# Holding the later loads back, and issuing weights earlier, in the start-up of a fused SSD and ReGLU kernel

## The chip, the cores and the metric

The kernel runs on one core of a Trainium2 chip. The metric is device time in microseconds, the median over several executions. A profiled execution gives the trace: which engine did what and when, how busy the 16 DMA engines of the core were, and which clock TensorE (the matmul engine) was granted. The other engines are VectorE (DVE in the profile), ScalarE (ACT), GpSimd (POOL) and SyncE (SP, which here only issues transfers).

## The reference, cut to what matters

Two stages follow each other. The first is a chunked state-space recurrence ("SSD") over 4 batches, 8 heads, 768 positions, head size 32 and state size 16; the second is a gated feed-forward layer on the result.

```python
# x: (4,8,768,32)  a: (4,8,768)  B, C: (4,8,768,16); chunk = 32
cum = cumsum(log a) within the chunk
L   = exp(cum_i - cum_j), lower triangle
y   = (C B^T * L) x  +  exp(cum_i) * C state
state = exp(sum log a) * state + sum_j exp(cum_end - cum_j) B_j x_j^T
# then, with x = y as (3072, 256), w_gate and w_val (256,1536), w_out (1536,256)
out = (maximum(x @ w_gate, 0) * (x @ w_val)) @ w_out
```

All inputs and the output are float32.

## The kernel before, in words

The kernel works on chunks of 128 positions, two at a time: a "pair" is 256 positions of one batch with all 8 heads, so there are 12 pairs and 3 per batch. The feed-forward layer works on blocks of 512 rows (two pairs) and 12 column blocks of 128 (`f` from 0 to 11). The decay is folded into B and C: both are multiplied by factors that come from running products of `a`, and what is left is a plain masked product.

For a pair p the steps are these. `load_bc` and `load_x` (or `load`) bring B, C and x into SBUF, all on SP's queue apart from some of the first ones, which ScalarE issues. `scale_wide` multiplies C (j = 1) or B (j = 0) by the factors, in two instructions each, on VectorE for pair 0 and on GpSimd for pairs 1 and 2. `cast_x` makes x bfloat16. `turn` transposes C and then B on TensorE, and `tevac` copies the result out of PSUM (tiles CT and BT). `G_wide` makes the products of C and B in four PSUM banks, `adds` the chunk's contribution to the state (it reads the cast x), `gmask` and `gcopy` mask and move the products, `carry` and `pass_on` hand the state on, `inter_wide` and `D_wide` make the output of the pair, and `yevac_wide` writes it transposed into yT.

`gvh(b, f, u)` is one column block of the first feed-forward product for half a row block (256 rows): two matmuls with the gate weights `wg`, two with the value weights `wv`, a ReLU on ScalarE and a product on VectorE. `gv` does the same for 512 rows. `fout` and `foevac` make the output. All of them share five PSUM banks.

The weights are read by GpSimd's queue, which also turns them into bfloat16: `weights(f0, f1)` issues one transfer for wg and one for wv, of 256 KB each for four column blocks; `weights_out` loads `w_out`.

The order of instructions on every engine is the order of the program: `in_order` adds a dependency from each instruction to the one before it on its engine. Each engine then runs its list strictly in turn, and an issue of a transfer is an instruction in the list of the engine that issues it. So the program text after line 623 is the schedule. `load_x(1, ...)` has one addition: it first sets one element of its tile by a `memset` on VectorE (line 94), and since the load overwrites that element, SP's issue waits for VectorE to get to this place in its list. All that follows on SP waits behind it.

The stretch at hand is the start-up: pair 0 goes through all its steps, pair 1 follows, and the first feed-forward blocks are put between them. In the program of before:

```python
    halves(0, 0, 0, 1)                       # column blocks 0, 1 of pair 0
    G_wide(1)
    adds(1)
    ...
    late = [gvh(0, 2, 0, True), gvh(0, 3, 0, True)]
    ...
    late += [gvh(0, 4, 0, True), gvh(0, 5, 0, True)]
    inter_wide(1)
    D_wide(1)
```

Of the kernel before, what the change touches and what calls it, by code (L numbers as in the profile page):

```python
# [29 lines left out]
def kernel(  # L30
# [13 lines left out]
    nc = tc.nc  # L44
# [34 lines left out]
    def load_bc(p, j, *qs):  # L79
        s = st.setdefault(p, {})  # L80
        if "bcr" not in s:
            s["bcr"] = raw.tile([128, NH, 2, 2, N], FP32, tag="bcr", name="bcr")
        n = NH // len(qs)
        for i, q in enumerate(qs):
            hs = slice(i * n, (i + 1) * n)
            q.dma_start(
                out=s["bcr"][:, hs, j].rearrange("p h r n -> p h (r n)"),
                in_=(B, C)[j][0, hs, p * 256:(p + 1) * 256, :].rearrange(
                    "h (p r) n -> p h (r n)", r=2))

    def load_x(p, *qs):
        xr = raw.tile([128, NH, 2, D], FP32, tag="xr", name="xr")
        if p == 1:
            nc.vector.memset(xr[0:1, 0, 0, 0:1], 0.0)
        n = NH // len(qs)
        for i, q in enumerate(qs):
            hs = slice(i * n, (i + 1) * n)
            q.dma_start(out=xr[:, hs].rearrange("p h r d -> p h (r d)"),
                        in_=x[0, hs, p * 256:(p + 1) * 256, :].rearrange(
                            "h (p r) d -> p h (r d)", r=2))  # L100
        st.setdefault(p, {})["xr"] = xr

    def load(p):
        q = nc.sync
        if p < NWIDE:
            load_bc(p, 1, q)
            load_bc(p, 0, q)
            load_x(p, q)
            return
        b, c0 = p // PPB, 2 * (p % PPB)  # L110
        xr = raw.tile([128, 2, NH, D], FP32, tag="xr", name="xr")
        bcr = raw.tile([128, 2, 2, NH, N], FP32, tag="bcr", name="bcr")
        for i in range(2):
            sl = slice((c0 + i) * 128, (c0 + i + 1) * 128)
            for src, j in ((B, 0), (C, 1)):
                q.dma_start(out=bcr[:, i, j], in_=src[b, :, sl, :].rearrange("h s n -> s h n"))
            q.dma_start(out=xr[:, i], in_=x[b, :, sl, :].rearrange("h s d -> s h d"))
        st[p] = {"xr": xr, "bcr": bcr}
# [69 lines left out]
    def weights(f0, f1):  # L188
        fs = slice(f0 * 128, f1 * 128)
        for w, src in ((wg, moe_w_gate), (wv, moe_w_val)):  # L190
            nc.gpsimd.dma_start(  # L191
                out=w[:, :, fs], in_=src[:, fs].rearrange("(k p) f -> p k f", k=2))
# [74 lines left out]
    def scale_wide(p, j, eng):  # L267
        s = st[p]
        if "bs" not in s:
            s["bs"] = bs = att.tile([128, 4, 128], BF16, tag="bs", name="bs")  # L270
            s["tin"] = [[bs[:, 2 * j + r] for r in range(2)] for j in range(2)]
        src = s["bcr"].rearrange("s (t q) j r n -> s j r t q n", t=2)[:, j]
        f = wfac[:, j, :, :, p]
        for t in range(2):
            eng.tensor_tensor(
                out=s["bs"][:, 2 * j:2 * j + 2].rearrange(
                    "s k (q t n) -> s k t q n", q=4, t=2)[:, :, t],
                in0=src[:, :, t],
                in1=f[:, :, 4 * t:4 * t + 4].to_broadcast([128, 2, 4, N]),
                op=ALU.mult)  # L280
# [16 lines left out]
    def cast_x(p, ceng):  # L297
        s = st[p]
        cast = ceng.copy if ceng is nc.scalar else ceng.tensor_copy
        xb = att.tile([128, 2 * NH * D], BF16, tag="xb", name="xb")  # L300
        if p < NWIDE:
            cast(xb, s["xr"].rearrange("s h r d -> s (h r d)"))
            s["xb"] = xb.rearrange("s (h r d) -> s h r d", h=NH, r=2)
        else:
            cast(xb, s["xr"].rearrange("s i h d -> s (i h d)"))
            s["x"] = [xb[:, i * NH * D:(i + 1) * NH * D] for i in range(2)]

    def transp(p, k, apart=False):

        s = st[p]  # L310
        if "tp" not in s:
            s["tp"] = {}
        if apart and k == 0:
            s["tp"][k] = bank("tpb", (128, 2, 128), BF16)
        elif not s["tp"]:
            tp = mm.tile([128, 2, 2, 128], BF16, tag="tp", name="tp")
            s["tp"] = {0: tp[:, 0], 1: tp[:, 1]}
        for i in range(2):
            nc.tensor.transpose(out=s["tp"][k][:, i], in_=s["tin"][k][i], identity=ident)  # L319
# [45 lines left out]
    def gmask(p, q, eng, psum=False):  # L365
        s = st[p]
        d = s["gw"][:, q]
        m = wmask.unsqueeze(2).to_broadcast([128, 2, 2, 128])
        eng.tensor_tensor(out=d, in0=s["gp"][q] if psum else d, in1=m, op=ALU.mult)

    def gcopy(p, q):
        s = st[p]
        nc.scalar.copy(out=s["gw"][:, q], in_=s["gp"][q])
# [259 lines left out]
    scale_wide(0, 1, V)  # L633
    nc.vector.reciprocal(wfac[:, 0, :, :, 0], wfac[:, 1, :, :, 0])
    scale_wide(0, 0, V)
    load_x(1, nc.sync)
    load(2)
    load(3)
    transp(0, 1, False)
    keep_warm(3)  # L640
    transp(0, 0, True)
    tevac(0, A_, V)
    nc.vector.reciprocal(wfac[:, 0, :, :, 1:3], wfac[:, 1, :, :, 1:3])
    scale_wide(1, 1, P_)
    scale_wide(1, 0, P_)
    weights(4, 8)
    cast_x(0, A_)
    keep_warm(4)
    G_wide(0)
# [1 line left out]
    keep_warm(19)  # L651
    gcopy(0, 0)
    gmask(0, 2, V, True)
    gcopy(0, 1)
    gmask(0, 3, V, True)
    gmask(0, 0, V)
# [192 lines left out]
```

## Time and profile before

| what | us |
|---|---|
| median of 7 runs (lowest to highest) | 131.19 (130.76 to 132.87) |
| the profiled execution's own time | 131.81 |
| its span | 130.1 |
| TensorE busy in the span | 122.3 |
| VectorE, ScalarE, GpSimd busy | 88.5, 81.9, 40.2 |
| mean granted TensorE clock | 0.987 of full speed |

Times in the trace count from the start of the span. In the timeline a row is start, duration, engine, line of the program, operation, output and inputs, and in brackets how long the engine sat idle before it and what ended that. A row can stand for several instructions (x2). "SPq" and "POOLq" are issues of transfers by SP and GpSimd; a transfer's landing is counted from its issue. The chain of waits goes back from the last instruction to what released it at each step. In the DMA view q0 is GpSimd's queue and q1 is SP's.

### The profile page before, as it was taken

The numbers are of one execution on the slowest core, as the hardware profiler recorded it, in microseconds if no ns is written. First come the engines' busy times: TensorE is split into PE (matmuls) and PEld (weight loads), VectorE is DVE, ScalarE is ACT, GpSimd is POOL, SyncE is SP. The second block draws the span as 40 slices with busy tenths as digits, with TensorE's granted clock in tenths as the row PEclk, the third lists the DMA queues.
The fourth block names the chain that finished last, engine by engine and source line by source line (L and its number), as shares of the span: only waits on it lengthen the run. The fifth ranks groups of instructions, "written<-read, shape, count | busy, mean of one in ns | idle before, by whom it ended". The sixth has DMA issues, their size and how long they took to land.

```text
span 130.1 us, 3446 instructions
## 1 busy us (share of the span) xinstructions
PE 122.3 (94%) x1294; PEld 85.0 (65%) x1294; DVE 88.5 (68%) x200; ACT 81.9 (63%) x186; POOL 40.2 (31%) x84
## 2 busy tenths in 40 slices
PE   6983999999999999999999999999999999999990
PEld 6751568667678567785558884477865577854770
DVE  4773675976399977468766778665799775687410
ACT  0554657863598874588744798844887845876310
POOL 6569941005375003390003670002930032000000
PEclk9999779999999999999999999999999999999999
DMA  4999999989797993269940186772200002200031
GB/s 71 200 178 195 208 196 205 108 96 128 81 168 136 117 104 51 85 121 122 103 63 27 53 156 73 96 88 83 86 0 0 0 5 81 81 0 5 0 109 53
DMA packets 72208, 12.14 MB, mean 93 GB/s; under 512 B 65936, under 2 KB 72192, under 8 KB 72192
## 3 DMA queue, kind: packets, MB, share of 16 engines
q1 hardware_dynamic: 66096, 8.91, 44.7%
q0 software_dynamic: 3184, 2.36, 12.2%
q10 hardware_dynamic: 2912, 0.66, 2.4%
q8 instruction: 10, 0.16, 0.5%
q14 instruction: 6, 0.05, 0.2%
HBM read 11.13 MB, written 3.15 MB: 110 GB/s over the span
## 4 chain that ended last, share of the span: by engine, by line
PE 86%; DMA 7%; DVE 2%; ACT 1%; POOL 1%; issue 0%; DVEq 0%; ACTq 0%
PE o L598 25%; PE gv L580 21%; PE gate L562 14%; PE val L565 14%; DMA wv<-in_moe_w_val_dram 6%; PE y L537 2%; PE g L463 2%; PE tp L319 2%; DMA a<-in_a_dram 2%; PE A_ps L500 1%; PE y L526 1%; POOL wg L191 1%; DVE h L586 1%; PE dec L246 1%; PE g L356 1%; ACT r L583 1%
## 5 line engine op out<-in xcount | busy, mean ns | idle before, releaser
L598 PE MATMUL o<-wo,h 128*128 128x256 bf16 x288 | 34.7, 273 | 0.0
L569 DVE TENSOR_TENSOR h<-r,val 128x512 bf16<-128x512 bf16 x42 | 28.3, 684 | 7.4 <-ACT r L568 6.4
L586 DVE TENSOR_TENSOR h<-r,gv 128x256 bf16<-128x256 bf16 x60 | 23.8, 420 | 10.0 <-ACT r L583 9.6
L598 PEld LDWEIGHTS <-h 128*128 128x128 bf16 x288 | 27.3, 98 | 5.0 <-issue 1.3
L568 ACT ACTIVATE r<-gate 128x512 bf16<-128x512 f32 x42 | 24.6, 601 | 6.4 <-PE gate L562 5.0
L583 ACT ACTIVATE r<-gv 128x256 bf16<-128x256 f32 x60 | 22.6, 384 | 5.1 <-PE gv L580 3.1
L471 POOL TENSOR_SCALAR_AFFINE_SELECT gs<-gs 128x512 bf16<-128x512 bf16 (+1 forms) x18 | 8.9, 521 | 54.2 <-ACT gs L482 54.2
L580 PE MATMUL gv<-yT,wv 128*128 128x256 bf16 x120 | 23.8, 282 | 1.9 <-DMA wv<-in_moe_w_val_dram 1.9
L562 PE MATMUL gate<-yT,wg 128*128 128x512 bf16 x84 | 25.0, 379 | 0.0
L565 PE MATMUL val<-yT,wv 128*128 128x512 bf16 x84 | 25.0, 379 | 0.0
L580 PE MATMUL gv<-yT,wg 128*128 128x256 bf16 x120 | 23.9, 282 | 0.5 <-DVE yT L454 0.4
L488 DVE TENSOR_TENSOR gs<-g,maskUT 128x512 bf16<-128x512 f32 x18 | 11.6, 686 | 10.4 <-issue 9.7
L565 PEld LDWEIGHTS <-wv 128*128 128x128 bf16 x84 | 8.2, 98 | 9.9
L580 PEld LDWEIGHTS <-wv 128*128 128x128 bf16 x120 | 12.1, 101 | 3.9 <-DMA wv<-in_moe_w_val_dram 2.1
L580 PEld LDWEIGHTS <-wg 128*128 128x128 bf16 x120 | 11.5, 100 | 3.2 <-issue 1.0
L562 PEld LDWEIGHTS <-wg 128*128 128x128 bf16 x84 | 7.8, 98 | 5.8
L289 POOL TENSOR_TENSOR bs<-bcr,scaleBC 128x256 bf16<-128x256 f32 x18 | 11.0, 630 | 0.0
L482 ACT CAST gs<-g 128x512 bf16<-128x512 f32 x9 | 5.3, 589 | 7.0 <-PE g L463 7.0
L614 ACT COPY ob<-o 128x512 f32<-128x512 f32 x10 | 5.8, 584 | 4.7 <-PE o L598 4.7
L550 ACT CAST yT<-y 128x512 bf16<-128x512 f32 x9 | 5.3, 586 | 5.5 <-PE y L537 5.3
L182 PE MATMUL w<-warm 128*128 128x128 bf16 x49 | 5.5, 287 | 1.0 <-DVE tmask L153 1.0
L508 DVE TENSOR_TENSOR Sm<-A_ps,smask 128x256 bf16<-128x256 f32 x15 | 6.2, 414 | 0.0
(99 smaller groups left out, 116.7 us busy)
## 6 DMA issues: line engine op xcount, KB each, us to landing
out_dram<-ob SPq DMA_DIRECT2D x10, 256.0 KB, 2.2
xr<-in_x_dram SPq DMA_DIRECT2D x19, 128.0 KB, 3.6
bcr<-in_C_dram SPq DMA_DIRECT2D x19, 64.0 KB, 3.4
bcr<-in_B_dram SPq DMA_DIRECT2D x19, 64.0 KB, 3.6
wg<-in_moe_w_gate_dram POOLq DMA_DIRECT2D x3, 256.0 KB, 5.7
wv<-in_moe_w_val_dram POOLq DMA_DIRECT2D x3, 256.0 KB, 7.4
wo<-in_moe_w_out_dram POOLq DMA_DIRECT2D x1, 768.0 KB, 11.9
xr<-in_x_dram SPq DMA_DIRECT2D x2, 256.0 KB, 8.6
```

The costliest lines, as they stand in the source:

```text
L289: eng.tensor_tensor(out=bs.rearrange("s k (q t n) -> s k t q n", q=4, t=2)[:, :, t], in0=src[:, :, t], in1=f[:, :, 4 * t:4 * t + 4].to_bro ...
L471: nc.gpsimd.affine_select(out=dst, in_=dst, pattern=[[0, n], [1, 128]], compare_op=ALU.is_ge, fill=0.0, base=0, channel_multiplier=-1)
L488: nc.vector.tensor_tensor(out=d[:, q], in0=g[q], in1=m, op=ALU.mult)
L508: nc.vector.tensor_tensor(out=n, in0=acc["A"], in1=smask, op=ALU.mult)
L562: nc.tensor.matmul(out=g, lhsT=wg[:, k, fs], rhs=yT[:, k, tk], start=(k == 0), stop=(k == 1))
L565: nc.tensor.matmul(out=v, lhsT=wv[:, k, fs], rhs=yT[:, k, tk], start=(k == 0), stop=(k == 1))
L568: nc.scalar.activation(r, g, AF.Relu)
L569: nc.vector.tensor_tensor(out=fst[b][:, f], in0=r, in1=v, op=ALU.mult)
L580: nc.tensor.matmul(out=gv_[:, j], lhsT=w[:, k, fs], rhs=yT[:, k, tk], start=(k == 0), stop=(k == 1), skip_group_check=True)
L583: nc.scalar.activation(r, gv_[:, 0], AF.Relu)
L586: nc.vector.tensor_tensor(out=fst[b][:, f, u * 256:(u + 1) * 256], in0=r, in1=gv_[:, 1], op=ALU.mult)
L598: nc.tensor.matmul(out=o[:, ts % 2], lhsT=fst[b][:, f, ts * 128:(ts + 1) * 128], rhs=wo[:, f], start=(f == 0), stop=(f == NF - 1), skip_gr ...
```

## The change

Two pieces of the program move; nothing is added or removed. The loads of x of pair 1 and of everything of pairs 2 and 3, which stood after the scaling of pair 0, now stand after the first masking of pair 0 on VectorE, and with them the memset that SP waits for. And the issue of the weights of column blocks 4 to 7 on GpSimd, which followed the scaling of both C and B of pair 1, now stands between the two.

```diff
     scale_wide(0, 0, V)
-    load_x(1, nc.sync)
-    load(2)
-    load(3)
     transp(0, 1, False)
     keep_warm(3)
     transp(0, 0, True)
     tevac(0, A_, V)
     nc.vector.reciprocal(wfac[:, 0, :, :, 1:3], wfac[:, 1, :, :, 1:3])
     scale_wide(1, 1, P_)
+    weights(4, 8)
     scale_wide(1, 0, P_)
-    weights(4, 8)
     cast_x(0, A_)
     keep_warm(4)
     G_wide(0)
...
     keep_warm(19)
     gcopy(0, 0)
     gmask(0, 2, V, True)
+    load_x(1, nc.sync)
+    load(2)
+    load(3)
     gcopy(0, 1)
     gmask(0, 3, V, True)
     gmask(0, 0, V)
```

The order on SP stays the same list; on VectorE the memset moves behind the C evacuation, a reciprocal and the first mask; on GpSimd the two issues move ahead of two scaling instructions. TensorE and ScalarE keep their lists.

## The prediction

> **What bounds the kernel now.** I read the page first (engine shares, chain), then the chain of waits from 4 to 20 us, the stages, the timeline of the moved instructions, and the DMA view in narrow stretches.
>
> ```profile
> PE 122.3 (94%) x1294; PEld 85.0 (65%) x1294; DVE 88.5 (68%) x200; ACT 81.9 (63%) x186; POOL 40.2 (31%) x84
> PE 86%; DMA 7%; DVE 2%; ACT 1%; POOL 1%; issue 0%; DVEq 0%; ACTq 0%
> ```
>
> TensorE is the bound nearly everywhere, and the one large stranger in the chain is a transfer, all of it in the first 15 us. The chain of waits of that stretch:
>
> ```profile
> 4.66 0.88 POOL wg L191
> 5.54 7.44 DMA wv<-in_moe_w_val_dram
> 12.99 0.05 issue
> 13.03 0.41 PE gv L580 x2
> ...
> 15.00 3.42 PE gv L580 x16
> ```
>
> TensorE waits for the value weights of blocks 0 to 3 (issued at 5.54, landed at 12.98). After that, 16 matmuls take 3.42 us, 0.214 each, where the same form later takes 0.107 (19.10 to 20.08: 0.98 for 8). The stages say why; columns are each engine's busy time, the granted clock, the DMA share and GB/s:
>
> ```profile
> 7.94:11.35 3.41, 2.42 (x61) 1.48 (x58) 2.98 (x8) 1.76 (x7) 3.41 (x7) 1.00 1.28 228
> 11.35:14.76 3.41, 1.46 (x37) 0.82 (x38) 0.84 (x2) 0.94 (x3) 3.41 (x7) 1.00 1.26 187
> 14.76:18.17 3.41, 3.41 (x35) 2.35 (x32) 2.87 (x8) 2.46 (x6) 2.81 (x11) 0.50 1.24 207
> 18.17:21.58 3.41, 3.41 (x74) 2.75 (x73) 1.79 (x5) 2.12 (x7) 0.17 (x1) 1.00 1.67 200
> ```
>
> A stretch in which TensorE was busy for 1.46 of 3.41 us is followed by one of the same length at half the clock. The wait is thus paid twice.
>
> The rows of the moved work, from the timeline (start, us, queue or engine):
>
> ```profile
> 5.57 0.37 SPq L98 DMA_DIRECT2D xr<-in_x_dram  x1
> 7.27 1.29 DVE L369 TENSOR_TENSOR gs<-g,wmask 128x512 bf16<-128x512 f32 x2 [0.88 <-PE g L356]
> 7.67 1.70 POOL L275 TENSOR_TENSOR bs<-bcr,wfac 128x128 bf16<-128x128 f32 x4 [1.40 <-DMA bcr<-in_C_dram]
> 9.31 0.76 POOL L191 DMA_DIRECT2D wg<-in_moe_w_gate_dram  x1
> 12.20 0.64 POOL L302 CAST xb<-xr 128x512 bf16<-128x512 f32 x1
> ```
>
> And the weights' queue (q0) beside SP's (q1), from the DMA view of 7.40 to 8.25, then 8.3 to 10.2, then 10.3 to 12.3:
>
> ```profile
> q0 software_dynamic: 124, 0.13, 95.2%
> ```
> ```profile
> q0 software_dynamic: 212, 0.20, 64.1%
> q1 hardware_dynamic: 1036, 0.26, 62.0%
> ```
> ```profile
> q1 hardware_dynamic: 1873, 0.24, 83.3%
> q0 software_dynamic: 154, 0.14, 51.2%
> ```
>
> In the first stretch SP moves nothing, although x of pair 1 was issued at 5.57: its packets come only after 8.25, when a_sb (issued at 3.89, landing 4.1 us later) is through. Then x (1024 packets), and after it C and B of pair 2, slow the weights: 146 packets per us alone (203 from 13.5 to 14.5), 112 beside x, 77 beside C and B.
>
> **The change, part by part.** *The hold.* The one-element memset (0.06 us) moves on VectorE from 5.46 to behind the first 0.65 us mask, which starts at 7.27. What stood behind it (the C evacuation, the reciprocal, that mask) gains 0.06 us, the second mask loses it: nothing on balance. SP issues x at about 8.0 instead of 5.57, 2.4 us later, and behind it in SP's order come C, B and x of pair 2 and all loads of pairs 3 to 5. But x's packets could not start before 8.25 anyway. SP's order itself does not change. With its queue empty at 8.0 and 0.8 to 1.2 us from issue to first packet (the first load is issued at 0.79, and the DMA view of 0 to 16 in slices of 0.4 us shows its first bytes in that of 1.6 to 2.0), they start near 9.1. The effective delay is 0.8 us, not 2.4.
>
> *Weights 0 to 3.* One transfer is 256 packets (256 KB, 1 KB each), both are 512. By 8.3 some 180 are through (47 from 6.4 to 7.4, 124, and a few). Before: 332 left, 212 go by 10.2, the other 120 at 77 per us until 11.75, and the last of the 16 engines lands 1.2 us later. After: 0.8 us more without SP, at 190 per us, leaves 180; at 112 per us they are through at 10.7, before C and B of pair 2 start (now near 11.1); with the same lag the landing is 11.9. Bounds: 10.7 (no lag) and 13.1 (the last engine is starved as before). I take 11.9.
>
> *B of pair 1 behind the weight issue.* POOL: C scaling 7.67 to 8.52 (half of 1.70), two issues (0.76, 0.72) to 10.0, B scaling to 10.85 instead of 9.37. The four transposes stand ahead of the first FFN matmul on TensorE: they ran at 10.04, now the two of B wait to 10.9, and the gate matmuls start near 11.05 instead of 10.80. It costs nothing as long as the value weights land after 11.25; were that cover gone, 0.25 us. The evacuations of B and C behind it (0.28, 0.85) end before the first ReLU. POOL's sum is unchanged: weights 8 to 11 issue at 10.85 as before, the cast of x of pair 1 at 12.2.
>
> *x of pair 1.* From issue to landing 5.4 us in the trace, 3.3 for the x issued at 27.91 in a quieter stretch: 11.3 to 13.4; first packet at 9.1 and 2.6 us of transfer (8.3 to 10.97 before) make 11.7, before POOL gets to the cast. At the late end the cast ends at 14.0 and the state matmuls (14.70 before) wait, which the next term covers.
>
> *What is late next: weights 4 to 7.* Issued 0.78 us earlier (8.52 and 9.28), but they queue behind 0 to 3 on a DMA that moves 187 to 228 GB/s in every stage, so it is the work ahead that decides. Their value half landed at 16.56 (10.06 + 6.5), 0.5 us before block 4 used it (17.04). After, the same packets lie ahead of it, apart from the part of x of pair 2 that slides behind: 0.2 to 0.3 us. Landing 16.3; bounds 15.5 (all of the issue's 0.78 and of x's share gained) and 16.9 (the queue idles). TensorE, starting at 11.9, has blocks 0 and 1, the G matmuls, blocks 2 and 3 and half of 4 done by about 14.85 (1.13 earlier than 17.04 less 1.06 for ten matmuls at 0.107 instead of 0.213), so it stops again, for 1.4 us. From 16.35 six matmuls at 0.107 are left before the inter-chunk products: 17.0 where the trace has 18.35.
>
> *Later loads.* C and B of pair 2 come 0.8 us later; their scaling on POOL (13.80) feeds transposes at 25.34. Pair 3's last x lands at 29.2 (25.15 + 4.0) for a cast at 33.18. The output weights land at 24.67 for a matmul at 28.19. All keep over 1.5 us: nothing.
>
> **Sum.** 18.35 - 17.0 = 1.35 us, and TensorE is full from there (3.41 of 3.41), so it stays. The profiled execution took 131.81 (span 130.10, 1.7 around it): 131.81 - 1.35 = 130.46. It stands 0.62 above the median of 131.19. The lowest run, 130.76, is 1.05 below, about what the half clock costs (block 4 could begin at 16.56 instead of 17.04, and six matmuls save 0.64): I estimate that the slow stretch falls differently from run to run. From that run only the 0.2 to 0.3 of the weights is left: 130.5 too.
>
> The Trainium skill, "TensorE: Matmul & The Clock Gate", Part 1, has a free-running window of 3.4 us, after an idle one of which the clock halves; the rows agree on the length (3.41), but halved it after a stretch 43% busy. By the page's rule of no gap over about 3 us, the after would never be halved and no run of before either.
> "DMA: Bandwidth & Descriptors", Rules for kernel authors, says to issue a DMA early and wait late, which speaks against holding x; by that rule the change gains nothing on the transfers and the time stays at 131.2.
>
> **Rivals.**
> 1. *The half clock moves to where it hurts (other side).* The new stop (14.85 to 16.3) may be answered by a half-clock stretch from about 16.5 to 19.9, where TensorE is the bound: 3.41 us at half cost 1.7. 131.81 - 1.35 + 1.7 = 132.2. For: 1.46 of 3.41 busy was punished. Against: around the new stop TensorE is busy 1.9 to 2.2 of 3.41, and 2.42 (7.94 to 11.35) was not. It decides once the stop is over about 1.3 us in one such stretch.
> 2. *Weights 0 to 3 land as before* (the last engine starved again, 13.0), and all else follows: 131.2. For: the last engine was 1.1 us behind the next stage already.
> 3. *Weights 4 to 7 land early too,* at 15.5 or before: 0.8 more, 129.7. Against: the full DMA.
> 4. *The holds cost more than the covers hide* (x at 13.4 and then late, weights 4 to 7 at 17.2): about 131.9.
>
> **Numbers.** Main case 0.45 (130.2 to 130.8), rival 1 0.16, rival 2 0.20, rival 3 0.12, rival 4 0.07. What a measurement tells from no change is 0.3%, 0.39 us: faster is under 130.80. Faster 0.57 (main and 3), same 0.19, slower 0.24 (1, 4, a little of 2). The range 129.7 to 132.0 leaves out part of 1 and of 3.
>
> **What would show it.** Value weights 0 to 3 landing at 11.3 to 12.3; first SP packets of x near 9.1; a new wait of TensorE on wv at block 4, ending at 16 to 16.7; inter-chunk products near 17.0. Wrong, if weights 0 to 3 still land at 13, if the 0.50 stretch lies after 16.5, or if the state matmuls wait for the cast beyond 16.

## The result, and the profile after

The changed kernel takes 130.23 us in the median (129.86 to 131.96, 26 runs), against 130.99 for the kernel before (130.5 to 133.31, 61 runs). The ratio is 0.9941 (95% interval 0.9928 to 0.9955): about 0.6% faster. The ratios, here and below, leave out executions that took over 1.5% longer than the fastest of their kernel; medians and ranges count all. The profiled execution took 130.14 (span 128.4), 1.67 less than the one of before that the prediction worked from.

First the chain of waits of the changed kernel (start, duration, what):

```profile
8.65 0.71 POOL wg L191
9.35 6.51 DMA wv<-in_moe_w_val_dram
15.86 0.05 issue
15.91 0.83 PE gv L580 x6
16.73 0.22 PE y L430 x8
```

The transfer in the chain is another one. Before it was the value weights of column blocks 0 to 3, landed at 12.98; now it is that of blocks 4 to 7, issued at 9.35 and landed at 15.86, and the six matmuls behind it run at full clock (0.83 for six, pipeline included) up to the inter-chunk products (L430). The stages, of the same length as those of before (after the window come its length, the busy times of the engines, the granted clock, the DMA share and GB/s):

```profile
11.54:14.95 3.41, 2.33 (x47) 1.59 (x45) 2.71 (x7) 2.14 (x5) 2.52 (x5) 1.00 1.14 169
14.95:18.36 3.41, 2.77 (x67) 1.93 (x66) 2.21 (x6) 2.46 (x8) 0.78 (x2) 1.00 1.39 221
```

TensorE is busy for 2.33 and 2.77 of 3.41 us where it had 1.46 before the half-clock stretch, and the clock stays at 1.00. The timeline shows where the moved work went, and three small waits on the way:

```profile
7.93 0.38 SPq L98 DMA_DIRECT2D xr<-in_x_dram  x1
10.93 0.29 PE L319 MATMUL tpb<-ident,bs 128*128 128x128 bf16 x2 [0.77 <-POOL bs L275]
11.27 0.38 PE L580 MATMUL gv<-yT,wv 128*128 128x256 bf16 x2
13.16 0.60 POOL L302 CAST xb<-xr 128x512 bf16<-128x512 f32 x1 [0.87 <-DMA xr<-in_x_dram]
13.82 0.21 PE L390 MATMUL y<-xb,bs 64*32 64x64 bf16 x4 [0.82 <-POOL xb L302]
15.91 0.39 PE L580 MATMUL gv<-yT,wv 128*128 128x256 bf16 x2 [0.64 <-DMA wv<-in_moe_w_val_dram]
```

The value matmuls of block 0 start at 11.27 without waiting. In place of the one long wait stand the late B of pair 1 (0.77), the late cast of x (0.82) and the weights of block 4 (0.64). The DMA view of the stretches 8.2 to 9.6 and 9.6 to 11.2 (q0 is the weights' queue, q1 SP's):

```profile
q0 software_dynamic: 280, 0.27, 121.4%
...
q1 hardware_dynamic: 1741, 0.34, 108.6%
q0 software_dynamic: 53, 0.04, 15.7%
```

Between 8.2 and 9.6 the weights have the DMA engines to themselves; x, issued at 7.93, and what follows it come after that, in a burst in which the weights get almost nothing. In the kernel before it was the other way round: x's packets already filled the first of these stretches (here from a profile of it at full clock, 8.2 to 9.6).

```profile
q1 hardware_dynamic: 935, 0.24, 75.9%
q0 software_dynamic: 118, 0.11, 47.6%
```

### The profile page after: what moved, and what is told of

The parts are those of the page before. It is cut to its first block, busy times and chain, and to the rows that moved or that the text cites. A ratio compares the mean times of both kernels' runs of the same rounds, so it can differ in the third digit from the quotient of the medians.

```text
span 128.4 us, 3447 instructions
## 1 busy us (share of the span) xinstructions
PE 121.0 (94%) x1294; PEld 84.6 (66%) x1294; DVE 89.3 (70%) x200; ACT 82.0 (64%) x186; POOL 40.3 (31%) x84
## 4 chain that ended last, share of the span: by engine, by line
PE 86%; DMA 5%; POOL 3%; issue 2%; DVE 1%; ACT 1%; DVEq 0%; ACTq 0%; POOLq 0%
PE o L598 25%; PE gv L580 19%; PE val L565 14%; PE gate L562 14%; DMA wv<-in_moe_w_val_dram 5%; PE y L537 2%; PE g L463 2%; PE tp L319 2%; PE w L182 2%; PE A_ps L500 1%; PE y L526 1%; POOL wg L191 1%; PE dec L246 1%; POOL bs L275 1%; POOL wv L191 1%
## 5 line engine op out<-in xcount | busy, mean ns | idle before, releaser
L580 PE MATMUL gv<-yT,wv 128*128 128x256 bf16 x120 | 22.9, 273 | 0.6 <-DMA wv<-in_moe_w_val_dram 0.6
L580 PE MATMUL gv<-yT,wg 128*128 128x256 bf16 x120 | 23.0, 273 | 0.2
L580 PEld LDWEIGHTS <-wv 128*128 128x128 bf16 x120 | 11.7, 98 | 2.3 <-DMA wv<-in_moe_w_val_dram 0.9
L580 PEld LDWEIGHTS <-wg 128*128 128x128 bf16 x120 | 11.2, 98 | 2.3 <-issue 0.5
```

Source lines behind the costliest of these rows:

```text
L580: nc.tensor.matmul(out=gv_[:, j], lhsT=w[:, k, fs], rhs=yT[:, k, tk], start=(k == 0), stop=(k == 1), skip_group_check=True)
```

## A clean pair: the kernel before at full clock

Two more profiles of the kernel before showed how far the first was an ordinary execution.

> The kernel before, unchanged, for one more look. Theory (the half clock after 14.76 in its first profile was a mishap of that execution, and what binds in most executions is the landing of the value weights 4 to 7): at full clock these land at 16.3 to 16.6, block 4 starts on that landing, inter-chunk products at 17.1 to 17.5, time 130.6 to 130.9. Rival (the half clock is regular): a stretch at half clock again after 13 us.

> The kernel before, unchanged, one more look. Theory (the last of the 16 engines makes the landing of the value weights 4 to 7 differ from execution to execution): landing at 16.2 to 17.5, inter-chunk products at least 0.8 behind it, time 130.6 to 131.8 without a half-clock stretch after 13 us. Rival (another wait sets the spread): inter-chunk products far from 0.8 behind the landing.

The first took 133.16, the second 130.83. The waits in the timeline of the first:

```profile
15.11 0.39 PE L580 MATMUL gv<-yT,wg 128*128 128x256 bf16 x2 [0.45 <-DMA wg<-in_moe_w_gate_dram]
17.59 0.61 PE L580 MATMUL gv<-yT,wv 128*128 128x256 bf16 x2 [2.08 <-DMA wv<-in_moe_w_val_dram]
```

and the stage behind it, half the clock on a stretch where TensorE is busy throughout:

```profile
17.41:20.82 3.41, 3.23 (x58) 2.00 (x59) 0.84 (x2) 1.40 (x4) 1.78 (x4) 0.50 1.68 202
```

So the half clock after a starved stretch comes back, as the rival had it, at another place, and here it is the prediction's first rival, on the kernel before. The second of the two (the third profile of the kernel) has no half-clock stretch in the start-up (mean clock 1.000):

```profile
11.79 0.39 PE L580 MATMUL gv<-yT,wv 128*128 128x256 bf16 x2 [0.71 <-DMA wv<-in_moe_w_val_dram]
16.64 0.39 PE L580 MATMUL gv<-yT,wv 128*128 128x256 bf16 x2 [1.03 <-DMA wv<-in_moe_w_val_dram]
17.52 0.28 PE L430 MATMUL Aps<-CT,Sw 32*32 32x128 bf16 x8
```

This execution is the fair partner of the changed kernel's: 130.83 against 130.14. Its first wait ends at 11.79, not at 13.03, and its second, for the value weights 4 to 7 (issued at 10.51, landed at 16.59), ends at 16.64 where the changed kernel has 15.91. That is 0.73, and the times differ by 0.69. In both kernels the weights of blocks 4 to 7 bind.

The trace also holds sixteen completion records for each of these transfers, taken here for one from each of the 16 DMA engines; the landing is the last of them. For the value weights 4 to 7:

| kernel | eighth engine | fourteenth | last |
|---|---|---|---|
| before, three profiles | 15.35, 16.14, 15.35 | 15.61, 16.36, 15.65 | 16.53, 17.54, 16.59 |
| hold alone | 14.59 | 14.99 | 16.08 |
| weights moved alone, two profiles | 14.91, 15.09 | 15.09, 15.24 | 16.70, 16.83 |
| changed kernel, two profiles | 14.95, 15.09 | 15.47, 15.45 | 15.86, 15.80 |
| pair 2 held longer, two profiles | 14.53, 14.73 | 15.02, 15.32 | 15.38, 15.57 |

So the theory of the last engine holds in part: it comes 0.9 to 1.2 behind the fourteenth in the kernel before, but in the execution that landed at 17.54 the other engines were late as well. In the changed kernel it comes 0.35 to 0.4 behind. Why is not shown.

## One number carries the time

The second inter-chunk group of pair 1 (the row "Aps<-CT,Sw" of L430) was read from every profile. In twelve of the fourteen the whole execution lasts 113.3 us longer, whatever was done ahead of it. In the other two the half clock was still on when the group ran (it ended at 20.8 in both):

| kernel | value matmul of block 4 | Aps<-CT,Sw | execution | difference |
|---|---|---|---|---|
| before, first profile | 17.04 | 18.47 | 131.81 | 113.34 |
| before, second profile | 17.59 | 19.16 | 133.16 | 114.00 |
| before, at full clock | 16.64 | 17.52 | 130.83 | 113.31 |
| before, with warming matmuls | 16.54 | 17.42 | 130.72 | 113.30 |
| weights moved alone | 16.75 | 17.72 | 132.22 | 114.50 |
| weights moved alone, again | 16.88 | 17.76 | 131.06 | 113.30 |
| hold alone | 16.13 | 17.01 | 130.31 | 113.30 |
| changed kernel | 15.91 | 16.79 | 130.14 | 113.35 |
| changed kernel, again | 15.85 | 16.73 | 130.02 | 113.29 |
| pair 2 held longer | 15.43 | 16.31 | 129.62 | 113.31 |
| pair 2 held longer, again | 15.61 | 16.50 | 129.86 | 113.36 |
| pair 2 held longer, x as before | 15.25 | 16.61 | 129.93 | 113.32 |
| weights 4 to 7 issued first | 18.11 | 19.25 | 132.57 | 113.32 |
| pair 2 held longest | 15.28 | 16.18 | 129.50 | 113.32 |

Where block 4 waits for its weights at full clock, the inter-chunk group stands 0.88 to 0.90 behind it. So where that wait binds, the landing of the value weights 4 to 7 sets the end, and nothing behind it took a gain back: the later loads of pairs 2 to 5, 0.8 us or more later, cost nothing.

## The experiments

**Each part alone.** The hold alone, with the weights of blocks 4 to 7 issued after both scalings as before:

```diff
 # against before
-    load_x(1, nc.sync); load(2); load(3)     # after scale_wide(0, 0, V)
 ...
     gmask(0, 2, V, True)
+    load_x(1, nc.sync); load(2); load(3)
```

> Hold alone: the loads of x of pair 1 and of pairs 2 and 3 wait for VectorE's first mask, and weights 4 to 7 are issued after both scalings, as before. Theory (the hold does it, by letting weights 0 to 3 through): weights 0 to 3 land near 10.7, the transposes of B of pair 1 do not wait, the value weights 4 to 7 land at 15.9 to 16.3, ratio to before 0.994 to 0.996. Rival (the earlier issue of weights 4 to 7 carries half of it): they land 0.75 later than in the changed kernel, 16.6, and the ratio is 0.997 or above.

Ratio 0.9951 (0.9919 to 0.9982), median 130.34. Its wait at block 4:

```profile
16.13 0.39 PE L580 MATMUL gv<-yT,wv 128*128 128x256 bf16 x2 [0.86 <-DMA wv<-in_moe_w_val_dram]
```

The weights 4 to 7 are issued 0.69 later than in the changed kernel (10.04 against 9.35) and land 0.22 later (16.08 against 15.86). The first theory's numbers hold. The transposes of B, which wait 0.77 in the changed kernel, do not wait here, and it makes no difference: the wait at block 4 covers it.

The weights alone:

```diff
 # against before
     scale_wide(1, 1, P_)
+    weights(4, 8)
     scale_wide(1, 0, P_)
-    weights(4, 8)
```

> Weights 4 to 7 between the scaling of C and B, loads as before. Theory: weights 0 to 3 still land at 13.0, weights 4 to 7 stay behind them in a full queue and land near 16.5; the late B of pair 1 is hidden behind the wait for weights 0 to 3; ratio 0.999 to 1.001. Rival (the earlier issue counts): weights 4 to 7 land at 15.8, ratio 0.996 to 0.998.

Ratio 0.9939 (0.9906 to 0.9972): no effect had been expected, and the theory fell. Its profile is of a slower execution (132.22, half clock from 17.4), with the weights 4 to 7 landing at 16.70. It was run again with a new theory.

> Weights 4 to 7 between the scaling of C and B, loads as before, once more. The first theory (no effect) fell with 0.994. New theory (supply: issued at 9.3 the weights 4 to 7 reach the DMA engines after weights 0 to 3 have run out on most of them; issued at 8.5 they follow without a gap): value weights 0 to 3 land at 11.5 to 13 as before, value weights 4 to 7 at 15.8 to 16.1 instead of 16.5, time equal to the changed kernel's within 0.2. Rival (the first ratio was chance): they land at 16.5 and the ratio is 0.997 to 1.

Ratio 0.9951 (0.9918 to 0.9985), so the first was no chance. But the profiled execution, at 131.06, is one of the slower ones of this kernel (its runs begin at 129.90), and in it the weights landed late:

```profile
15.35 0.39 PE L580 MATMUL gv<-yT,wg 128*128 128x256 bf16 x2 [0.70 <-DMA wg<-in_moe_w_gate_dram]
16.88 0.39 PE L580 MATMUL gv<-yT,wv 128*128 128x256 bf16 x2 [1.14 <-DMA wv<-in_moe_w_val_dram]
```

So neither profile shows the earlier landing that the supply theory wants. The reports of the single engines go some way towards it: fifteen of the sixteen were done by 15.11 and 15.25, against 16.01 in the kernel before at full clock, and in both executions the last came 1.6 behind them. Whether it comes sooner in the executions that make the ratio is not shown, and so in what way the earlier issue alone gains 0.5% stays open.

By these ratios each part alone gives most of the gain of both (0.995, and 0.994 to 0.995, against 0.9941). But each interval reaches 0.3% to either side, so half of it is not excluded, nor that the two add up. The executions at full clock alone, each kernel beside the kernel before on the same chip, say rather less for each part: medians 0.38 below the kernel before for the hold (130.34 against 130.72), 0.38 and 0.56 for the weights (130.34 against 130.72, 130.44 against 131.00), and 0.89 for both together (130.11 against 131.00).

**Is the half clock what was gained?** The kernel before, its wait untouched, with TensorE kept busy during it by matmuls on the constant warm tile:

```diff
 # against before, in gvh, for column block 0 of pair 0 alone
         for j, w in ((0, wg), (1, wv)):
+            if j == 1 and nwarm:
+                keep_warm(nwarm)             # 28 matmuls
```

> The kernel before with 28 additional matmuls on the constant warm tile put between the gate and the value matmuls of column block 0, where TensorE waits for the weights; nothing else changes and the wait stays. Theory (the wait is paid a second time by the half clock): no stretch at half clock after 11 us, block 4 starts on the landing of weights 4 to 7 at 16.5, inter-chunk products near 17.2 instead of 18.35, ratio 0.996 to 0.998 and less scatter. Rival (the half clock is hidden behind the wait for weights 4 to 7 in most runs): ratio 0.999 to 1.001.

Ratio 0.9982 (0.9952 to 1.0012), median 130.70: not to be told from no change, and so no decision between the two. The profiled execution ran without a half-clock stretch after 11 us, with the inter-chunk group at 17.42; the kernel before did the same without help in its third profile (17.52). In the first profile the half clock cost about a microsecond (18.47 against 17.52).

The mean clock is on record for executions without a trace too, and it settles more: a stretch like that of the first profile leaves 0.987, and no execution of these kernels lies between 0.987 and 0.994. Below 0.99 were 26 of the 64 executions of the kernel before that ran beside the variants, none of the 12 with warming matmuls, and 5 of 38 of the changed kernel. Of the others, the kernel before has a median of 130.72 on the chip of this experiment, the same as with warming, and of 131.00 on the chip where the changed kernel has 130.11. So the change gains at full clock too, and the median's gain is not the half clock's. That the half clock comes more rarely is a second effect, seen in the slowest executions.

**The changed kernel again**, beside the others on one chip:

> The changed kernel, unchanged, beside the others on one chip. Both theories: ratio to before 0.993 to 0.996, value weights 4 to 7 at 15.7 to 16.1, inter-chunk products 0.8 after that.

Ratio 0.9947 (0.9917 to 0.9977); block 4 at 15.85.

**Can the weights be brought in sooner?** Two ways. One holds the loads of pairs 2 and 3 until VectorE has evacuated pair 0 (10.8), by a memset on the first tile of pair 2, as the change does it for x:

```diff
 # against the changed kernel
     load_x(1, nc.sync)
-    load(2)
-    load(3)
 ...
     yevac_wide(0, A_, V)
+    load(2)                                  # with a one-element memset of its B/C tile on VectorE
+    load(3)
```

> The changed kernel with the loads of pairs 2 and 3 held further, until VectorE has evacuated pair 0 (near 10.5); x of pair 1 stays where the change put it. Theory (in the changed kernel the wait for the value weights 4 to 7, ended at 15.9, is what binds, and C and B of pair 2 are what delays them): C and B come 0.5 to 0.8 later, the weights land at 15.2 to 15.6, inter-chunk products at 16.1 to 16.4 instead of 16.66, time 0.25 to 0.5 below the changed kernel, ratio to before 0.990 to 0.993. Rival (the cast of x of pair 1, ended at 13.8, binds): same as the changed kernel, 0.994.

> The same kernel as the one with the loads of pairs 2 and 3 held until pair 0 is evacuated, once more, beside its variants on one chip. Theory (the landing of the value weights 4 to 7 binds, and C and B of pair 2 are what delays it): landing 15.2 to 15.6, ratio to before 0.986 to 0.991. Rival (the first ratio came from few runs): 0.993 to 0.996, as the changed kernel.

Ratios 0.9883 (0.9848 to 0.9918) and 0.9900 (0.9875 to 0.9924), both intervals below that of the changed kernel. In the first profile the weights 4 to 7 landed at 15.4 (9.19 + 6.2):

```profile
10.87 0.37 SPq L86 DMA_DIRECT2D bcr<-in_C_dram  x1
13.54 0.21 PE L394 MATMUL y<-xb,bs 64*32 64x64 bf16 x4 [0.64 <-POOL xb L306]
15.43 0.39 PE L584 MATMUL gv<-yT,wv 128*128 128x256 bf16 x2 [0.44 <-DMA wv<-in_moe_w_val_dram]
```

Against the changed kernel block 4 starts 0.48 earlier and the execution is 0.52 shorter. The cast of x of pair 1 (0.64 of waiting) does not bind. In the second profile they landed at 15.57, still 0.29 before those of the changed kernel.

The other way issues the weights 4 to 7 at once behind 0 to 3, with the same hold:

```diff
 # against the kernel above
     weights(0, 4)
+    weights(4, 8)
 ...
     scale_wide(1, 1, P_)
-    weights(4, 8)
     scale_wide(1, 0, P_)
```

> The changed kernel with weights 4 to 7 issued directly behind weights 0 to 3, before any scaling, and the loads of pairs 2 and 3 held until VectorE has evacuated pair 0. Theory (the landing of the value weights 4 to 7 sets the end, at 0.8 before the inter-chunk products): they land at 14.2 to 14.9 and stop binding; what binds then is the cast of x of pair 1 (13.8 in the changed kernel) and the ten and six matmuls behind it, 15.7 to 16.0; time 0.2 to 0.5 below that of the kernel with only the loads held further (129.65). Rival (the DMA is full, so the order of issue does nothing): 129.6 to 129.7.

Both theories missed: ratio 1.0162 (1.0074 to 1.025), from two of the six executions (132.57 and 133.97); the other four took 135.49 to 136.31. All six have a mean clock below 0.99. The profile is of the fastest. x of pair 1, issued at 8.06, found the weights' queue full. The DMA view from 7.4 to 9.5, from 9.6 to 11.5 and from 11.7 to 13.7, and then the row of TensorE's wait:

```profile
q0 software_dynamic: 407, 0.40, 118.6%
...
q0 software_dynamic: 371, 0.35, 114.2%
...
q0 software_dynamic: 235, 0.22, 69.8%
q1 hardware_dynamic: 880, 0.22, 53.5%
```

```profile
15.76 0.24 PE L394 MATMUL y<-xb,bs 64*32 64x64 bf16 x4 [3.14 <-POOL xb L306]
16.00 0.61 PE L584 MATMUL gv<-yT,wg 128*128 128x256 bf16 x2
```

Not one packet of SP moves in the first two stretches, 3.5 us after the issue. The cast of x comes late, TensorE waits 3.14, and the matmuls behind it run at half clock (0.61 for two). The weights 4 to 7 landed at 14.1, close to the 14.2 that the theory began at, and that is worth nothing then. It is the first half of the prediction's fourth rival (x late), brought about by going too far, and it shows what the place between the two scalings is good for: the weights 4 to 7 are not yet in the queue when x asks for its turn.

**Which of the held loads matters?** x of pair 1 back at its old place, the loads of pair 2 held as above:

```diff
 # against "pair 2 held longer"
     scale_wide(0, 0, V)
+    load_x(1, nc.sync)
 ...
     gmask(0, 2, V, True)
-    load_x(1, nc.sync)
```

> As that kernel, but x of pair 1 is issued where it stood before the change (near 5.6); C, B and x of pair 2 and all behind them wait until pair 0 is evacuated (near 10.8). Theory (of the loads that the change holds, C and B of pair 2 cost, x does not): value weights 0 to 3 land at 11 to 11.7, x of pair 1 by 10.8, no wait for its cast, value weights 4 to 7 at 15.0 to 15.6, ratio 0.986 to 0.992. Rival (holding x is what counts): value weights 4 to 7 at 15.8 to 16.5, ratio 0.994 or above.

Ratio 0.9892 (0.9863 to 0.9921), the same as with x held. The weights 0 to 3 landed at 12.2, later than expected; x shares the DMA with them again, but fourteen engines were done by 11.2, and the last two took until then. The weights 4 to 7 landed at 14.7, and block 4 no longer waits for them: in this execution the chain goes through the weights 0 to 3.

```profile
5.60 6.56 DMA wv<-in_moe_w_val_dram
```

So once C and B of pair 2 are held, holding x brings nothing that can be measured.

**How far does it go?** The loads of pairs 2 to 5 held until VectorE has made the products of blocks 0 and 1:

```diff
 # against the changed kernel: load(2), load(3), load(4), load(5) now stand here, memset as above
     halves(0, 0, 0, 1)
+    load(2); load(3); load(4); load(5)
```

> As that kernel, x of pair 1 as in the change, with the loads of pairs 2 to 5 held further, until VectorE has made the products of column blocks 0 and 1 (near 12.9). Theory: value weights 4 to 7 land at 14.5 to 15.1 and bind no more or just so; inter-chunk products at 15.6 to 15.9, ratio 0.984 to 0.988. Rival (the loads become late themselves: scaling of pair 2 on GpSimd after 22.5 and the transposes of pair 2 wait): 0.990 to 0.996.

Ratio 0.9868 (0.9835 to 0.9902), median 129.51; the interval lies below that of the changed kernel. It rests on four of its six executions; the other two took 131.07 and 131.22, at a mean clock of 1.000, so the half clock is not what slowed them. The timeline shows that this is the end of the road:

```profile
15.28 0.39 PE L584 MATMUL gv<-yT,wv 128*128 128x256 bf16 x2 [0.20 <-DMA wv<-in_moe_w_val_dram]
22.27 0.78 POOL L279 TENSOR_TENSOR bs<-bcr,wfac 128x128 bf16<-128x128 f32 x2 [1.91 <-DMA bcr<-in_B_dram]
23.06 0.39 PE L323 MATMUL tp<-ident,bs 128*128 128x128 bf16 x4
```

Block 4 waits for 0.20 only, and the scaling of B of pair 2 ends at 23.05, the very moment at which TensorE comes to transpose it (23.06). By these rows a longer hold would be a wait there. Whether the two slower executions had such a wait is not known, for neither has a trace; counted in, they leave the median at 129.51.

## Why the prediction was right, and where not

The forecast was 130.5 with a range of 129.7 to 132.0; 130.23 was measured. By its steps:

- *What bounds.* Right for the execution it was read from, but half of what it showed was that execution: the landing at 12.98 and the half clock after it are absent from the third profile of the same kernel (11.79, clock 1.000). The prediction's guess that the slow stretch falls differently from run to run is borne out (14.76 in one, 17.4 in another, none in the third). That the fastest runs owe their time to that is true in part at most: at full clock alone executions on one chip spread from 130.31 to 131.51, and two with a mean clock of 0.984 and 0.986 took only 130.46 and 130.49.
- *The sum.* That it came near is in part luck. It takes 1.35 from an execution that was 0.98 slower than one at full clock (131.81 against 130.83), and most of that 1.35 is the half clock and the late landing of that one execution, which the usual one does not have. For an execution without them the prediction allowed 0.2 to 0.3; measured were 0.69 between the profiles and 0.76 between the medians.
- *The hold's effective delay.* Predicted: x's packets near 9.1, 0.8 later than before. Measured: after 9.6, 1.3 or more later than the 8.25 of before; from 8.2 until then the DMA view shows the weights' packets alone. x landed at 13.0 (7.93 + 5.1) instead of 11.7, near the late bound of 13.4, the cast ran at 13.16 and TensorE waited 0.82 for it. The sentence that the next term would cover this was right: the wait at block 4 remained.
- *Weights 0 to 3.* Predicted 11.9, measured 10.7 (5.48 + 5.2), the early bound. The lag of 1.2 for the last engine was carried over from the one profile of before, where it came at 12.99, 1.08 behind the fifteenth; in the changed kernel it came 0.20 behind. And 494 of the 512 packets were through by 9.6 (214 from 6.4 to 8.2, then 280), before x moved, so that the slower rate beside x hardly entered.
- *B of pair 1.* Predicted 10.85 for the scaling and 10.9 for the transposes; measured 10.88 (10.09 + 0.79) and 10.93. The cover that it named (value weights after 11.25) was gone, and the later one took its place.
- *Weights 4 to 7.* The step that was mis-sized. Predicted landing 16.3, a gain of 0.2 to 0.3 over a full-clock execution of before; measured 15.86, 0.73 earlier than 16.59. It was reckoned from packets that must pass in any case, and for most of the engines that is about right: the eighth reported at 14.95 instead of 15.35, the fourteenth at 15.47 instead of 15.65. What the sum left out is the last engine, 0.94 behind the fourteenth in that execution of before and 0.39 in the changed kernel. Had this been seen, the forecast from the fast runs would have been 130.1.
- *From block 4 to the end.* Right: predicted six matmuls, then 17.0; measured 16.73 for the first inter-chunk group, and 113.3 from the second group to the end wherever the half clock was over by then.
- *Rivals.* No half clock behind the new stop in the profile of the changed kernel (1.00 in its stages, the stop 0.64 instead of 1.4); rival 1 appeared in a run of before. But 5 of 38 executions of the changed kernel have a mean clock of 0.982 to 0.987 and took 131.10 to 132.26, near the 132.2 of that rival; where their half clock fell is not known, for none has a trace. Rival 2 (weights 0 to 3 late again) did not come: 10.7. Rival 3 (weights 4 to 7 at 15.5 or before) is what the longer holds made of it: 15.4 and 15.2, 129.6 and 129.5.

The two rules of the Trainium skill that were weighed: "TensorE: Matmul & The Clock Gate" (Part 1) takes an idle window for the halving; here a stretch that was 43% busy was followed by half the clock, and so was, in the second profile of before, one busy for 0.75 of 3.10 us. "DMA: Bandwidth & Descriptors" (Rules for kernel authors) says to issue early; here holding loads that nobody needs yet made the kernel 0.5% and, held longer, 1.0 to 1.3% faster. Issuing the weights 4 to 7 a little earlier gained 0.5% too, as the rule has it; issuing them earliest made it 1.6% slower.

## What to carry to other kernels

When the DMA engines are full, the order in which transfers are issued is a schedule: hold a load whose reader comes late until the one that TensorE waits for has passed, and look whether the next reader in line still gets its data in time. Hold by small steps: here a hold up to the end of blocks 0 and 1 still paid, with nothing to spare behind it. Read the size of a wait from more than one profile before a sum is built on it; find the moment behind which the rest of the execution has a fixed length, and compare kernels at that moment.

## What was not expected of the hardware

The landing of the same transfer differs between executions of one kernel: value weights 0 to 3 at 12.98 in one and near 11.7 in the two others, value weights 4 to 7 at 16.53, 16.59 and 17.54. Much of that can be a single engine: of the value weights 0 to 3 fifteen engines were done by 11.91, 11.52 and 11.59, the sixteenth at 12.99, 11.62 and 11.74. And while the weights' queue had much ahead of it, SP's queue moved nothing: x of pair 1 had no packet for some 1.7 us after its issue behind two weight transfers and for 3.5 us behind four. Once it moved in the changed kernel, the weights got 53 packets beside 1741. How the engines share between the queues was not tested further.
